# Half of a diagonal block read back turned instead of formed, and another order of steps, in an attention and expert kernel

## The chip, the cores and the metric

The kernel runs on one core of a Trainium2 chip. The metric is the device time of one execution in microseconds; a time is the median of several runs. The engines are named as in the profile: PE is TensorE's matmul side and PEld its weight loads, ACT is ScalarE, DVE is VectorE, POOL is GpSimd, and SP is SyncE, which here issues nearly all DMAs.

## The reference

A batch of 8 sequences of 2496 rows goes through an attention with squared ReLU and no softmax; its output goes, row by row, to one of 8 experts. All of it is float32.

```python
scores = (1.0 / S) * np.matmul(z, z.transpose(0, 2, 1))   # z: 8 x 2496 x 64
attn = np.maximum(scores, 0.0) ** 2
x = (u * np.matmul(attn, v)).reshape(B * S, D)            # D = 256
logits = x @ w_gate + modality_bias[modality_id]
e_idx = np.argmax(logits, axis=1)
# for the rows of each expert e:
out[mask] = gate_w[mask, None] * (np.maximum(x[mask] @ w1[e], 0.0) @ w2[e])
```

The scores come from z on both sides, so the matrix of squares is symmetric: block (q, c) is block (c, q) turned.

## The kernel before

The kernel has two stages. The first, up to about 1287 us, does the attention and the routing; the second runs the experts over tiles of 512 rows and is not touched by the change.

**Tiling of the attention.** A sequence is cut into `NCH` = 5 chunks of 512 queries (the last one 448). Within a chunk (b, c) there are `NI` = 10 steps; step i covers two tiles of 128 keys, 2i and 2i + 1, and so half of key chunk i // 2. Steps 2c and 2c + 1 of chunk c are the diagonal block, where query chunk and key chunk are the same.

**What a step does.** A step that is formed fresh goes through these pieces: `scores` (line 300) makes six matmuls on PE, three for each of the two row halves of the array, with 64 rows of z as weights and up to 512 query columns; `root` (line 317) takes the ReLU out of PSUM on ACT into a tile from the pool `a` (six buffers, named r); `square` (line 359) squares it there. Then `high` (line 386) casts it to ah on ACT or DVE, `low` (line 395) makes the rest al on DVE, and `weigh` (line 409) multiplies ah and al with the two parts of V in 24 matmuls (line 425) that add up in the accumulators acc. The pools ah and al have four buffers each. The score pool s in PSUM has one.

**Squares that are read back.** For key chunks below the query chunk (q < c) the squares have been formed already, in chunk q, with queries and keys the other way round. There, `turn_squares` (line 334) transposes the tile on DVE in blocks of 32 into one of two buffers turn, and `store_squares` (line 342) writes it in four DMAs (six for the last step) to `squares[q, c]` in DRAM. In chunk c, `load_turned` (line 325) reads it back in place of scores, root and square. `turns` says for which pairs this is done.

**Order.** `order_of` (line 277) sets the order of the steps of a chunk: turned steps, called late, and fresh ones are spread evenly among each other, with step 9 last. For chunks 0 to 3 that is

```
chunk 0: 0 1 2 3 4 5 6 7 8 9
chunk 1: 2 0 3 4 5 6 1 7 8 9
chunk 2: 0 4 5 1 6 2 7 3 8 9
chunk 3: 0 6 1 2 7 3 4 8 5 9
```

The order of instructions on each engine is written by a planner that runs when the kernel is built (lines 1120 to 1197). Each piece has an engine, a cost in us, a due time `need` counted in steps, the pieces that it comes after, and the buffers that it takes and gives back. The planner keeps a clock for each engine and gives an engine the piece with the earliest due time that is ready by these clocks. Scores are due `LEAD` = 3.6 steps ahead of their products, and a turned read 2.5 steps before that. SP issues DMAs in the order so planned, through eight lanes: a DMA waits until the one eight places earlier has landed.

## Time and profile before

| what | value |
|---|---|
| median of 3 runs | 2191.28 us (2191.19 to 2193.09) |
| the profiled execution's own time | 2189.61 us |
| its span, first to last instruction | 2187.7 us |
| PE, DVE, ACT busy in the span | 2168.1, 1612.7, 1404.0 us |
| score matmuls (line 314) | 1452 records, 217.3 us busy |
| products (line 425) | 9360 records in three groups of 3120 |
| DMA queue of SP (q1) | 329.58 MB, 58.8% of the 16 engines' span |

The busy time of PE includes matmuls that overlap, and their ends are modelled; what a matmul costs is read from the distance of starts. Matmuls on 64 rows run in pairs, one in each row half of the array. A row of the list of waits names who waited, for whom, and for how long in total, how often, and at the longest.

### The profile page before, as it was taken

To read this page: it belongs to the slowest core of one execution; us is meant where nothing else is said; L and a number is where in the kernel's file an instruction comes from. 1 tells how busy PE (TensorE), PEld (TensorE's weight loads), DVE (VectorE), ACT (ScalarE), POOL (GpSimd) and SP (SyncE) were. 2 spreads that over 40 slices of the span, in tenths; PEclk is the share of its full clock that TensorE was granted. 3 is DMA by queue.
4 is the path that set the end of the run, shared out by engine and by line. 5 is a ranking of instruction groups with operands and counts; after the bars stand their busy time and mean duration, and the time that the engine had idled before them with its cause. 6 is when DMAs were issued, how large, how long until landed. Compare 5 with 4: busy or idle time off the path is not lost. (4 is left out here: it accounts for less than half of the span.)

```text
span 2187.7 us, 42980 instructions
## 1 busy us (share of the span) xinstructions
PE 2168.1 (99%) x16550; PEld 1879.4 (86%) x16550; DVE 1612.7 (74%) x2231; ACT 1404.0 (64%) x1978; POOL 360.3 (16%) x342
## 2 busy tenths in 40 slices
PE   9999999999999999999999999999999999999997
PEld 7888888899998898888888888888888888888886
DVE  8779768778878878778788756666666666666664
ACT  8768768768768677678778753555455555555553
POOL 0000310300300300301302403212121211111121
PEclk9999999999999999999999999999999999999999
DMA  7975976967958958957948833645454544545450
GB/s 176 256 208 119 249 216 145 250 203 155 281 162 176 277 150 180 294 137 168 274 117 173 208 105 102 178 122 168 116 163 127 150 139 135 155 129 161 124 159 24
DMA packets 587874, 373.63 MB, mean 171 GB/s; under 512 B 488426, under 2 KB 543210, under 8 KB 581898
## 3 DMA queue, kind: packets, MB, share of 16 engines
q1 hardware_dynamic: 572570, 329.58, 58.8%
q0 software_dynamic: 15088, 41.21, 5.0%
q8 instruction: 132, 2.16, 0.4%
q14 instruction: 84, 0.69, 0.1%
HBM read 246.49 MB, written 140.96 MB: 177 GB/s over the span
## 5 line engine op out<-in xcount | busy, mean ns | idle before, releaser
L401 DVE TENSOR_TENSOR al<-r,ah 128x1024 fp32r<-128x1024 f32 (+1 forms) x359 | 424.3, 1190 | 56.3 <-ACT ah L392 52.0
L425 PE MATMUL acc<-ah,vh 64*128 64x512 f32 (+1 forms) x3120 | 451.2, 386 | 0.1
L1237 PE MATMUL po<-w,hh 128*128 128x512 f32 x1248 | 448.2, 396 | 2.3 <-issue 2.3
L425 PE MATMUL acc<-al,vh 64*128 64x512 f32 (+1 forms) x3120 | 439.4, 382 | 0.0
L425 PE MATMUL acc<-ah,vl 64*128 64x512 f32 (+1 forms) x3120 | 438.5, 383 | 0.0
L1228 ACT ACTIVATE hh<-ph 128x512 fp32r<-128x512 f32 x312 | 186.1, 597 | 379.4 <-PE ph L1224 379.3
L1224 PE MATMUL ph<-xh,w 128*128 128x512 f32 x1248 | 427.2, 393 | 0.6 <-DVE x L485 0.6
L1229 DVE SCALAR_TENSOR_TENSOR hl<-ph,hh 128x512 fp32r<-128x512 f32 x312 | 215.6, 691 | 230.6 <-ACT hh L1228 230.5
L640 POOL DMA_INDIRECT xs<-x,sloti x160 | 202.5, 1266 | 1064.9 <-ACT ah L392 772.0
L322 ACT ACTIVATE r<-s 128x1024 f32<-128x1024 f32 (+2 forms) x244 | 247.0, 1013 | 173.1 <-PE s L314 166.8
L425 PEld LDWEIGHTS acc<-al,vh 64*128 64x128 f32 x3120 | 319.6, 185 | 40.8
L425 PEld LDWEIGHTS acc<-ah,vh 64*128 64x128 f32 x3120 | 317.1, 185 | 43.5 <-ACT x L481 0.7
L1238 PE MATMUL po<-w,hl 128*128 128x256 f32 x1248 | 350.4, 281 | 0.1
L425 PEld LDWEIGHTS acc<-ah,vl 64*128 64x128 f32 x3120 | 313.6, 185 | 41.9
L392 ACT CAST ah<-r 128x1024 fp32r<-128x1024 f32 (+1 forms) x268 | 272.5, 1031 | 32.0 <-PE acc L425 26.4
L1237 PEld LDWEIGHTS po<-w,hh 128*128 128x128 f32 x1248 | 234.7, 188 | 57.1 <-issue 2.7
L1224 PEld LDWEIGHTS ph<-xh,w 128*128 128x128 f32 x1248 | 234.7, 188 | 55.3 <-PE ph L1224 1.0
L1247 POOL DMA_INDIRECT out_dram<-y,ids x157 | 152.7, 973 | 752.7 <-DVE y L1275 725.6
L368 ACT ACTIVATE r<-r 128x1024 f32<-128x1024 f32 (+2 forms) x243 | 255.9, 1054 | 6.0
L1224 PE MATMUL ph<-xl,w 128*128 128x512 f32 x624 | 245.8, 394 | 0.3 <-DVE xl L866 0.3
L1238 PEld LDWEIGHTS po<-w,hl 128*128 128x128 f32 x1248 | 235.5, 189 | 9.6 <-DVE hl L1229 0.4
L339 DVE STREAM_TRANSPOSE turn<-r 128x1024 f32<-128x1024 f32 x158 | 196.0, 1241 | 45.8 <-ACT r L368 27.7
(159 smaller groups left out, 2177.3 us busy)
## 6 DMA issues: line engine op xcount, KB each, us to landing
squares<-turn SPq DMA_DIRECT2D x508, 128.0 KB
r<-squares SPq DMA_DIRECT2D x96, 512.0 KB
w<-w1s SPq DMA_DIRECT2D x37, 1024.0 KB
w<-w2s SPq DMA_DIRECT2D x37, 1024.0 KB
r<-squares SPq DMA_DIRECT2D x62, 448.0 KB
ut<-in_ut_dram SPq DMA_DIRECT2D x40, 512.0 KB
xg<-xs SPq DMA_DIRECT2D x156, 128.0 KB
vr<-in_v_dram SPq DMA_DIRECT2D x32, 512.0 KB
```

The costliest lines, as they stand in the source:

```text
L322: nc.scalar.activation(out=r[:, t, :w], in_=s[t][:, :w] if g < 2 else s[:, :, :w], func=AF.Relu, scale=INV)
L339: nc.vector.transpose(out=y.rearrange(order, n=2), in_=st_a[g].rearrange("p n (t i) -> p n t i", i=BLK))
L368: nc.scalar.square(out=a[:, t, :w], in_=r[:, t, :w])
L392: copy(out=ah[:, :, :w], in_=st_a[g][:, :, :w])
L401: nc.vector.tensor_tensor(out=al[:, :, :w], in0=a[:, :, :w], in1=ah[:, :, :w].bitcast(F32), op=ALU.subtract)
L425: nc.tensor.matmul(out=acc[b, c][r][dh][:, :w], lhsT=V[b, k // J][y][halves[r], k % J, dh * P:(dh + 1) * P], rhs=x[halves[r], k % 2, :w], ...
L640: nc.gpsimd.indirect_dma_start(out=xs, out_offset=bass.IndirectOffsetOnAxis(ap=RT[b]["sloti"][:n, k:k + 1], axis=0), in_=x[:n, j, :], in_o ...
L1224: nc.tensor.matmul(out=ph, lhsT=lhs, rhs=rhs[:, k, :], start=n == 0, stop=n == 3 * KD - 1)
L1228: nc.scalar.activation(out=hh, in_=ph, func=AF.Relu)
L1229: nc.vector.scalar_tensor_tensor(out=hl, in0=ph, scalar=0.0, in1=hh.bitcast(F32), op0=ALU.max, op1=ALU.subtract)
L1237: nc.tensor.matmul(out=po[j], lhsT=hh[:, s], rhs=both, start=f == 0, stop=False, skip_group_check=True)
L1238: nc.tensor.matmul(out=po[j][:, 0:D], lhsT=hl[:, s], rhs=w[:, 0, :], start=False, stop=f == KF - 1, skip_group_check=True)
```

## The change

The pairs (c, c) for c = 0 to 3 get a place in DRAM too. In those chunks, but for chunk 0 of the first batch, the two diagonal steps no longer do the same work. The first one, 2c, is the source: it is formed whole, and the half of its query columns that belongs to the keys of the other step (columns 256 to 511) is transposed and stored. The second one, 2c + 1, is halved: `scores`, `root` and `square` make only columns 256 to 511, and `load_turned` reads columns 0 to 255 into the same tile. `high`, `low` and `weigh` then work on the whole tile as before. A halved step therefore has both a read and scores.

The order of steps changes with it: the source comes first or second in its chunk and the halved step stands seventh.

```
chunk 0: 0 2 3 4 5 6 1 7 8 9
chunk 1: 0 2 4 5 6 1 3 7 8 9
chunk 2: 0 4 1 6 2 7 5 3 8 9
chunk 3: 0 6 1 2 3 4 7 8 5 9
```

The due times of the source's transpose and stores are moved ahead (n - 1.5 and n - 1.4 instead of n + 0.5 and n + 0.4, counted from its own step n).

```diff
@@ -69,6 +69,7 @@
     w1s = dram.tile([E, P, KD, F], F32, name="w1s")
     w2s = dram.tile([E, P, KF, D], F32, name="w2s")
     places = dram.tile([MAXT, 2], I32, name="places")
+    pairs |= {(c, c) for c in range(NCH - 1)}
     squares = {(q, c, e): dram.tile([T, T], F32, name=f"squares{q}_{c}_{e}") for q, c in pairs for e in range(2)}
 
 
@@ -270,16 +271,27 @@
 
 
     NI = NCOL // 2
+    HALF_AT = 6
 
     def turns(b, q, c):
         return q < c and (q, c) in pairs and (b < B - 1 or q < NCH - 2)
 
+    def halved(b, c):
+        return c < NCH - 1 and b + c > 0
+
     def order_of(b, c):
 
         late = [i for i in range(NI) if turns(b, i // 2, c)]
         fresh = [i for i in range(NI - 1) if i not in late]
-        n = len(late) + len(fresh)
-        return sorted(late + fresh, key=lambda i: (late.index(i) + 0.4) / len(late) if i in late else (fresh.index(i) + 0.6) / len(fresh)) + [NI - 1]
+        at = {i: (n + 0.4) / len(late) for n, i in enumerate(late)}
+        at.update({i: (n + 0.6) / len(fresh) for n, i in enumerate(fresh)})
+        order = sorted(at, key=at.get)
+        if halved(b, c):
+            order.remove(2 * c)
+            order.remove(2 * c + 1)
+            order.insert(1 if late else 0, 2 * c)
+            order.insert(HALF_AT, 2 * c + 1)
+        return order + [NI - 1]
 
     steps = [(b, c, i) for b in range(B) for c in range(NCH) for i in order_of(b, c)]
     first_step = {(b, c): order_of(b, c)[0] for b in range(B) for c in range(NCH)}
@@ -293,6 +305,17 @@
             return x[:, j * P:(j + 1) * P]
         return x[:, j // 2 * H:(j // 2 + 1) * H].rearrange("p (k n) -> p n k", n=2)[:, j % 2]
 
+    def is_half(g):
+        b, c, i = steps[g]
+        return halved(b, c) and i == 2 * c + 1
+
+    def is_source(g):
+        b, c, i = steps[g]
+        return turns(b, c, i // 2) or halved(b, c) and i == 2 * c
+
+    def columns(g):
+        return slice(H if is_half(g) else 0, width[steps[g][1]])
+
     def is_turned(g):
         b, c, i = steps[g]
         return i // 2 < c and turns(b, i // 2, c)
@@ -300,7 +323,7 @@
     def scores(g, more=False):
 
         b, c, i = steps[g]
-        w = width[c]
+        w = columns(g)
         if more:
             s = [bank_tile([P, T], "s") for _ in halves]
         else:
@@ -311,21 +334,24 @@
             for t in range(2):
                 k = 2 * i + t
                 lhs = key_columns(Z[b, k // J][halves[t], kl], k)
-                nc.tensor.matmul(out=s[t][:, :w], lhsT=lhs, rhs=mv[halves[t], ql, :w], start=n == 0, stop=n == 2)
+                nc.tensor.matmul(out=s[t][:, w], lhsT=lhs, rhs=mv[halves[t], ql, w], start=n == 0, stop=n == 2)
         st_s[g] = s if more or not g else both
 
     def root(g):
-        w = width[steps[g][1]]
+        w = columns(g)
         s = st_s.pop(g)
-        r = bulk.tile([P, 2, T], F32, tag="a", bufs=NA, name="r") if g else first_root
+        if is_half(g):
+            r = st_a[g]
+        else:
+            r = bulk.tile([P, 2, T], F32, tag="a", bufs=NA, name="r") if g else first_root
         for t in range(2) if g < 2 else (slice(0, 2),):
-            nc.scalar.activation(out=r[:, t, :w], in_=s[t][:, :w] if g < 2 else s[:, :, :w], func=AF.Relu, scale=INV)
+            nc.scalar.activation(out=r[:, t, w], in_=s[t][:, w] if g < 2 else s[:, :, w], func=AF.Relu, scale=INV)
         st_s[g] = r
 
     def load_turned(g):
 
         b, c, i = steps[g]
-        w = width[c]
+        w = H if is_half(g) else width[c]
         a = bulk.tile([P, 2, T], F32, tag="a", bufs=NA, name="r")
         src = squares[i // 2, c, b % 2].rearrange("(s p k) q -> s p k q", s=2, k=2)
         nc.sync.dma_start(out=a[:, :, :w], in_=src[i % 2, :, :, :w])
@@ -336,7 +362,9 @@
         b, c, i = steps[g]
         y = raw.tile([P, T // BLK, 2 * BLK], F32, tag="turn", bufs=2, name="turn")
         order = "p t (i n) -> p n t i" if i < NI - 1 else "p t (n i) -> p n t i"
-        nc.vector.transpose(out=y.rearrange(order, n=2), in_=st_a[g].rearrange("p n (t i) -> p n t i", i=BLK))
+        t = slice(H // BLK if i == 2 * c else 0, T // BLK)
+        x = st_a[g].rearrange("p n (t i) -> p n t i", i=BLK)
+        nc.vector.transpose(out=y.rearrange(order, n=2)[:, :, t], in_=x[:, :, t])
         st_t[g] = y
 
     def store_squares(g):
@@ -348,7 +376,8 @@
             mine = y[n * BLK:(n + 1) * BLK]
             if i < NI - 1:
                 k0 = i % 2 * H + n * 2 * BLK
-                nc.sync.dma_start(out=dst[:, :, k0:k0 + 2 * BLK], in_=mine)
+                t = slice(H // BLK if i == 2 * c else 0, T // BLK)
+                nc.sync.dma_start(out=dst[:, t, k0:k0 + 2 * BLK], in_=mine[:, t])
             else:
                 for k in range(2 if n < 2 else 1):
                     k0 = (J // 2 + k) * P + n * BLK
@@ -357,7 +386,7 @@
     roots = {}
 
     def square(g):
-        w = width[steps[g][1]]
+        w = columns(g)
         a = r = st_s.pop(g)
         if g < 2:
 
@@ -365,7 +394,7 @@
             roots[g] = r
         for t in (range(2),) if g else ((0,), (1,)):
             t = slice(t[0], t[-1] + 1)
-            nc.scalar.square(out=a[:, t, :w], in_=r[:, t, :w])
+            nc.scalar.square(out=a[:, t, w], in_=r[:, t, w])
         st_a[g] = a
 
     def first_high(g):
@@ -890,7 +919,7 @@
         return p
 
     def piece(on, us, need, f, *args, after=(), take=(), drop=(), gate=-1):
-        p = Piece(on, us, need, f, args, [d if isinstance(d, tuple) else (d, 0.1) for d in after if d], list(take), drop, gate)
+        p = Piece(on, us, need, f, args, [d for d in (d if isinstance(d, tuple) else (d, 0.1) for d in after) if d[0]], list(take), drop, gate)
         pieces.append(p)
         return p
 
@@ -949,34 +978,37 @@
         b, c, i = steps[n]
         f = scale[c]
         high_after = None
-        hold_a = Hold("a", 1 + turns(b, c, i // 2))
-        if is_turned(n):
-            src = [stored[b, i // 2, 2 * c + k] for k in range(2)]
-            p = transfer(1.4, n - LEAD - 2.5, load_turned, n, after=src, take=[hold_a], gate=n - LEAD - 4)
-            high_after = (p, 0.2)
-        elif n >= MADE:
+        hold_a = Hold("a", 1 + is_source(n))
+        read = None
+        if is_turned(n) or is_half(n):
+            src = [stored[b, i // 2, 2 * c + k] for k in range(1 if is_half(n) else 2)]
+            read = transfer(0.7 if is_half(n) else 1.4, n - LEAD - 2.5, load_turned, n, after=src, take=[hold_a], gate=n - LEAD - 4)
+            high_after = (read, 0.2)
+        if not is_turned(n) and n >= MADE:
+            f /= 1 + is_half(n)
             hold_s = Hold("s")
             p = piece(
                 "P", 0.69 * f, n - LEAD, scores, n, after=[done_z.get((b, c)), done_z.get((b, i // 2)), scored.get("last")],
                 take=[hold_s], drop=[hold_z[k] for k in {(b, c), (b, i // 2)}],
             )
             scored["last"] = (p, 0.0)
-            p = piece("A", 0.95 * f + 0.06, n - LEAD + 0.3, root, n, after=[(p, 0.25)], take=[hold_a], drop=[hold_s])
+            p = piece("A", 0.95 * f + 0.06, n - LEAD + 0.3, root, n, after=[(p, 0.25), (read, -20.0)], take=() if read else [hold_a], drop=[hold_s])
             p = piece("A", 0.95 * f + 0.06, n - LEAD + 1.0, square, n, after=[p])
+            f = scale[c]
             high_after = (p, 0.08)
         if n > 0:
             own = n in (1,)
             p = piece(
                 "D" if own else "AD", 1.3 if own else 0.93 * f, n - 1.8, high, n,
-                after=[high_after, split.get("high")], take=[Hold("ah")],
+                after=[high_after, (read, 0.2), split.get("high")], take=[Hold("ah")],
                 drop=[Hold("a")] if n == 1 else (),
             )
             split["high"] = (p, 0.0)
             hold_h = [p.take[0], Hold("al")]
-            if turns(b, c, i // 2):
+            if is_source(n):
                 hold_t = Hold("turn")
-                t = piece("D", 1.18, n + 0.5, turn_squares, n, after=[high_after], take=[hold_t], drop=[hold_a])
-                stored[b, c, i] = transfer(2.8, n + 0.4, store_squares, n, issues=4 if i < NI - 1 else 6, after=[t])
+                t = piece("D", 0.62 if i == 2 * c else 1.18, n - 1.5 if i == 2 * c else n + 0.5, turn_squares, n, after=[high_after], take=[hold_t], drop=[hold_a])
+                stored[b, c, i] = transfer(1.4 if i == 2 * c else 2.8, n - 1.4 if i == 2 * c else n + 0.4, store_squares, n, issues=4 if i < NI - 1 else 6, after=[t])
                 later.append((stored[b, c, i], hold_t))
                 begun.append(stored[b, c, i])
             p = piece(
@@ -1141,7 +1173,7 @@
             need = {}
             for h in p.take:
                 need[h.pool] = need.get(h.pool, 0) + 1
-            if p.f in (load_turned, root) and free["a"] <= sum(n not in held for n in range(step_now + 1, p.args[0])):
+            if p.f in (load_turned, root) and p.args[0] not in held and free["a"] <= sum(n not in held for n in range(step_now + 1, p.args[0])):
                 return False
             return all(free[k] >= n for k, n in need.items())
 
```

How the change stands on the engines, at three places of the fifth batch (b = 4). The rows have the line, the instruction, its output and inputs by the program's names, and its shape; lines of the changed kernel are some twenty to thirty higher. On PE, chunk 0, the seventh group of score matmuls of that chunk, before:

```order
L425 MATMUL acc<-al,vh 128x512 x8
L314 MATMUL s<-zm 128x512 x6
L425 MATMUL acc<-ah,vh 128x512 x8
L425 MATMUL acc<-ah,vl 128x512 x8
L425 MATMUL acc<-al,vh 128x512 x8
L314 MATMUL s<-zm 128x512 x6
```

and now:

```order
L454 MATMUL acc<-al,vh 128x512 x8
L337 MATMUL s<-zm 128x256 x6
L454 MATMUL acc<-ah,vh 128x512 x8
L454 MATMUL acc<-ah,vl 128x512 x8
L454 MATMUL acc<-al,vh 128x512 x8
L337 MATMUL s<-zm 128x512 x6
```

The six matmuls there have 256 columns instead of 512; the products around them are the same in number and shape. On SP, around the end of chunk 2 and the first half of chunk 3 (r is a tile of squares, vr, ut and w1s are the loads of V and U and the laying out of the experts' weights), before:

```order
L355 DMA squares2_4_0_66<-turn_11006 32x16x32 x6
L331 DMA r_11049<-squares2_3_0_78 128x1024
L157 DMA vr_11082<-in_v_dram 128x1024
L331 DMA r_11129<-squares2_3_0_78 128x1024
L157 DMA vr_11132<-in_v_dram 128x1024
L268 DMA ut_11145<-in_ut_dram 128x1024
L218 DMA w1s_61<-in_moe_w1_dram 16x4096
L331 DMA r_11226<-squares0_4_0_70 128x2x448
```

and now:

```order
L384 DMA squares2_4_0_66<-turn_11079 32x16x32 x6
L357 DMA r_11164<-squares2_3_0_82 128x1024
L219 DMA w1s_61<-in_moe_w1_dram 16x4096
L380 DMA squares3_3_0_86<-turn_11188 32x8x64 x4
L158 DMA vr_11230<-in_v_dram 128x1024
L158 DMA vr_11249<-in_v_dram 128x1024
L357 DMA r_11276<-squares2_3_0_82 128x1024
L269 DMA ut_11290<-in_ut_dram 128x1024
L219 DMA w1s_61<-in_moe_w1_dram 16x4096
L357 DMA r_11319<-squares3_3_0_86 128x2x256
L357 DMA r_11373<-squares0_4_0_70 128x2x448
```

The four stores of the source (squares3_3, 8 blocks of 32 instead of 16) and the read of the half are new; five other DMAs stand between them. On DVE, chunk 3, before (turn is a transpose, al a low part, x and rl belong to the output of the chunk before, lg to the routing):

```order
L534 TENSOR_REDUCE lg_10384<-sums_11228 128x32
L638 COPY x_9555<-side_10237 128x2
L339 STREAM_TRANSPOSE turn_11304<-r_11294 128x2x512
L401 TENSOR_TENSOR al_11334<-r_11294,ah_11302 128x1024
L401 TENSOR_TENSOR al_11340<-r_11129,ah_11332 128x1024
L339 STREAM_TRANSPOSE turn_11381<-r_11375 128x2x16x32
L403 TENSOR_TENSOR al_11411<-r_11375,ah_11379 128x512
```

and now:

```order
L531 TENSOR_TENSOR rl_11321<-x_11215,rh_11288 128x1024
L667 COPY x_9670<-side_10270 128x2
L430 TENSOR_TENSOR al_11328<-r_11164,ah_11317 128x1024
L563 TENSOR_REDUCE lg_10477<-sums_11375 128x32
L421 CAST ah_11438<-r_11319 128x1024
L430 TENSOR_TENSOR al_11441<-r_11319,ah_11438 128x1024
L367 STREAM_TRANSPOSE turn_11469<-r_11435 128x2x512
L430 TENSOR_TENSOR al_11475<-r_11435,ah_11443 128x1024
L430 TENSOR_TENSOR al_11481<-r_11276,ah_11473 128x1024
```

The cast of the halved step's tile r_11319, which needs the read, stands on DVE, and its low part, the transpose of the next step and that step's low part come after it. In the whole program there are 186 score matmuls of 256 columns and 1158 of 512 (1344 of 512 before), 31 transposes of half size, and 115 casts of ah on DVE (130 before) beside 283 on ACT (268 before).

## The prediction

> **What bounds the kernel now.** I read the page first, then the list of TensorE's waits, then the busy time of one batch split into its five chunks (each stretch begins at a chunk's first product), and last the timeline of TensorE.
>
> ```profile
> span 2187.7 us, 42980 instructions
> PE 2168.1 (99%) x16550; PEld 1879.4 (86%) x16550; DVE 1612.7 (74%) x2231; ACT 1404.0 (64%) x1978; POOL 360.3 (16%) x342
> ...
> PE po L1237 <- issue: 2.3, 1, 2.3
> PE s L314 <- ACT zm L230: 1.9, 1, 1.9
> PE warm L1101 <- POOL zeros L101: 1.0, 1, 1.0
> PE s L314 <- DVE zm L235: 0.6, 1, 0.6
> PE ph L1224 <- DVE x L485: 0.6, 1, 0.6
> PE ph L1224 <- DVE xl L866: 0.3, 1, 0.3
> ```
>
> Busy 99% alone would prove little, since ends of matmuls are modelled; the six waits do. In the whole span PE waited 6.7 us, and none of it for the pieces ah and al of the attention's squares, nor for a read of turned squares. The chunks of the fourth batch:
>
> ```profile
> 492.30:527.80 35.50, 35.50 (x329) 35.19 (x328) 31.45 (x41) 31.09 (x43) 0.00 (x0) 1.00 0.78 164
> 527.80:561.30 33.50, 33.50 (x316) 33.50 (x314) 27.88 (x47) 28.45 (x37) 7.19 (x6) 1.00 0.81 186
> 561.30:593.10 31.80, 31.80 (x298) 31.80 (x297) 25.87 (x36) 21.57 (x30) 10.68 (x9) 1.00 1.02 292
> 593.10:623.50 30.40, 30.40 (x286) 30.40 (x285) 22.09 (x28) 15.66 (x24) 9.08 (x7) 1.00 0.86 251
> 623.50:652.60 29.10, 29.10 (x299) 29.10 (x297) 23.25 (x28) 22.11 (x33) 0.00 (x0) 1.00 0.39 128
> ```
>
> After the length come PE, PEld, DVE, ACT, POOL, the granted clock and the DMA share. PE is full in all five at a clock of 1.00. DVE is nearest behind it in chunk 0 (31.45 of 35.50), and the DMA engines are full in chunk 2. So **time taken from PE's stream in the attention stage is time taken from the kernel**, as long as operands stay ahead. Whether the stream itself is dense, the timeline tells (start, length, form, count):
>
> ```profile
> 577.80 0.33 PE L514 MATMUL po<-mover,rh 64*128 64x80 f32 x2
> 577.91 0.33 PE L514 MATMUL po<-mover,rl 64*128 64x80 f32 x2
> 578.02 1.00 PE L314 MATMUL s<-zm 64*128 64x512 f32 x6
> ...
> 581.53 0.89 PE L314 MATMUL s<-zm 64*128 64x512 f32 x6
> 582.21 1.12 PE L425 MATMUL acc<-ah,vh 64*128 64x512 f32 x8
> ...
> 584.93 1.12 PE L425 MATMUL acc<-ah,vh 64*128 64x512 f32 x8
> 585.84 1.12 PE L425 MATMUL acc<-ah,vl 64*128 64x512 f32 x8
> ...
> 1700.26 0.28 PE L1238 MATMUL po<-w,hl 128*128 128x256 f32 x1
> 1700.38 0.40 PE L1237 MATMUL po<-w,hh 128*128 128x512 f32 x1
> ```
>
> Starts count here, not lengths. Six score matmuls, three pairs in the two row halves, take 582.21 - 581.53 = 0.68 us: 0.227 a pair. Eight products take 0.91, the same 0.227. No gap is left to win except by fewer columns.
>
> **The change, part by part.** *Scores.* The second diagonal step of chunks 0 to 3, without chunk 0 of the first batch, forms 256 columns: 8 x 4 - 1 = 31 steps, 93 pairs. The order has them as 186 matmuls of 128x256 and leaves all other matmuls in number and shape. No row shows a pair of 64-row matmuls of 256 columns, so it is bounded. From below by the pair of 80 columns, two loads included: 577.91 - 577.80 = 0.11 us. From above by the full width's own 0.227, no gain. The row nearest in width is the 256-column matmul over 128 rows: 1700.38 - 1700.26 = 0.12 us. The trace thus has the same column count at 0.12, and the same number of loads at 0.11; **I take 0.118**. A pair saves 0.109 us, a step 0.327, and 31 steps **10.1 us**; with 0.11 it would be 10.9, at the upper end 0.
>
> The pair's two weight loads are what could spoil this. The Trainium skill (TensorE: Matmul & The Clock Gate, section LDWEIGHTS (loading the stationary operand)) says that a load's time goes by columns, not rows: columns over 1.2, an estimate of 107 ns for 128. Two such loads in a row would hold a pair at 213 ns, and by that rule the sum would be 93 x 0.013 = 1.2 us. The trace disagrees where it can: in the 80-column rows two matmuls with two loads start every 0.11 us, so the loads of the two row halves overlap there.
>
> *ScalarE and VectorE.* The groups by line:
>
> ```profile
> L401 DVE TENSOR_TENSOR al<-r,ah 128x1024 fp32r<-128x1024 f32 (+1 forms) x359 | 424.3, 1190 | 56.3 <-ACT ah L392 52.0
> L322 ACT ACTIVATE r<-s 128x1024 f32<-128x1024 f32 (+2 forms) x244 | 247.0, 1013 | 173.1 <-PE s L314 166.8
> L392 ACT CAST ah<-r 128x1024 fp32r<-128x1024 f32 (+1 forms) x268 | 272.5, 1031 | 32.0 <-PE acc L425 26.4
> L368 ACT ACTIVATE r<-r 128x1024 f32<-128x1024 f32 (+2 forms) x243 | 255.9, 1054 | 6.0
> L339 DVE STREAM_TRANSPOSE turn<-r 128x1024 f32<-128x1024 f32 x158 | 196.0, 1241 | 45.8 <-ACT r L368 27.7
> ```
>
> A halved step takes half of a root and of a square from ACT, about 0.51 + 0.53 = 1.0 us, 32 in all, which I cost at nothing gained since PE never waited for it. The high and low parts stay whole. DVE gains 31 half transposes, between 0.62 (half of 1.241) and 1.24 us each; by size I take 0.62: 19 us over the stage. PE's own work covers it. In chunk 0 DVE goes from 31.45 of 35.50 to 32.1 of 35.2, 91%; at the upper end 93%. That producers run ahead shows in L392: 26.4 of its 32.0 us of idling ended with PE's products, which free the ah buffers. If the cover went, the price would be at most the transposes, 19 us, less the ACT time that the planner can hand over; the order already has 15 casts of ah moved from DVE to ACT (115 instead of 130 on DVE), 15 x 0.68 us back by DVE's rate.
>
> *DMAs.* Each halved step adds four stores of 64 KB and one read of 256 KB, 155 issues on SP. It adds a chain as well: the read needs the stores of the source step of the same chunk. What SP and the lanes give:
>
> ```profile
> 611.64 2.21 SPq L351 DMA_DIRECT2D squares<-turn  x4
> ...
> r<-squares SPq DMA_DIRECT2D x5, 512.0 KB
> squares<-turn SPq DMA_DIRECT2D x12, 128.0 KB
> vr<-in_v_dram SPq DMA_DIRECT2D x2, 512.0 KB
> zr<-in_zt_dram SPq DMA_DIRECT2D x3, 256.0 KB
> squares<-turn SPq DMA_DIRECT2D x10, 64.0 KB
> w2s<-in_moe_w_dram SPq DMA_DIRECT2D x2, 256.0 KB
> ut<-in_ut_dram SPq DMA_DIRECT2D x1, 512.0 KB
> ...
> SPq L331 <- DMA squares<-turn: 7.9, 13, 2.1
> ACT ah L392 <- DMA r<-squares: 1.2, 2, 0.6
> ```
>
> The seven rows in the middle are SP's issues in the fullest stretch, chunk 2: 35 in 31.8 us. With eight lanes at most eight are in flight, so a transfer is in flight 8 x 31.8 / 35 = 7.3 us on average at most. The chain, with its upper ends: root 1.01, square 1.05, transpose 1.24, four issues 2.21, flight of the stores 7.3, flight of the read 7.3, cast 1.03, low part 1.19: 22.3 us. Against it stands PE's work between the source's scores and the halved step's first product. It is shortest in chunk 3; there the order has 93 pairs of products, 16 of 80 columns, 6 of full scores and 3 of half ones: 21.1 + 1.8 + 1.4 + 0.35 = 24.6 us. The low part comes eight pairs (1.8 us) later still. **So the read is hidden, by 2 us where it is tightest**; in chunks 0 to 2 the same count gives about 26 us or more. What remains is that SP stands at the read until the stores have landed, with the next stores behind it; reads that waited for stores so far did it 13 times, 2.1 us at worst. The two turn buffers, and DVE's next transpose, wait behind those stores. I take nothing for it, from a bound of 31 x 2.1 us of SP time, because PE has DVE's lead before it.
>
> *Order.* The first step of chunks 1 is now a turned one, and the source comes second. From a step's scores to its first product PE has as much work between as before (6.1 us at the least then, 6.5 now, by counting the order's rows). That is worth nothing, within 2 us.
>
> *Sum.* 2189.61 us of the profiled execution less 10.1 is 2179.5. The median of the three runs lies 1.7 above that execution, so the forecast is 2191.28 - 10.1 = **2181.2 us**.
>
> **The rivals.** *Loads bind.* The loads of a 64-row pair run one behind the other where matmuls are short. By the 128-row row, one load and its matmul every 0.12 us, two are 0.24, over the 0.227 of a full pair: nothing is gained, 2191.3 us; halfway, at 0.17 a pair, it would be 2186. For it: that row is the only one of 256 columns. Against it: the 80-column pairs. The Trainium skill's rule on weight loads (TensorE: Matmul & The Clock Gate), weighed above, speaks for this rival.
>
> *The reads come late.* The one that ends slower. The DMA engines are at 1.02 and 0.86 in chunks 2 and 3, and there the change adds 0.5 MB each to 292 GB/s x 31.8 us = 9.3 MB and 251 x 30.4 = 7.6 MB. If stores and read each fly 3 us longer, the chain to the cast's end is 28.3 - 1.2 = 27.1 against 24.6 and about 26: the 8 products of chunk 3 start 2.5 us late, the 8 of chunk 2 1.1 us, 29 us together, and the time is 2210. It is slower by more than 0.2% from 14.5 us on (10.1 eaten, 4.4 over), 0.9 us of lateness in each. For it: the full share. Against it: all 158 reads of before made ACT wait 1.2 us in total, and chunk 4, at 0.39, lets the queue drain.
>
> *Operands come later here and there.* A lead that shrinks by a step in chunk 0, where DVE is fullest, or in chunk 3: 0.6 us in each of the 8 batches, 5 us, 2186. Against it: the 26.4 us above.
>
> *The change doesn't do what it says*: excluded, since the order has the 256-column matmuls, half transposes and half reads, and no root in it waits for the read of its own tile.
>
> **How the numbers follow.** A measurement of this kernel tells about 0.2%, 4.4 us, from no change. Forecast 0.72; operands late 0.13; loads bind 0.09; reads late 0.06. The forecast alone spans 2180 to 2183 (10.9 to 8.5 us). Faster takes the forecast and most of the third case, 0.83; same takes the loads and a rest, 0.12; slower 0.05, as the reads may also be late by less. The range, 2179 to 2187, adds the third case and the spread of the runs, and leaves the other two out.
>
> **What would show it.** Right: scores of 256 columns that start 0.35 us before what follows; PE's list of waits still without ah, al and r<-squares; chunks 0 to 3 shorter by 0.33 us each, and chunk 4 and everything behind 1287 us as long as before. Wrong in the first term: 0.6 us or more from a half score to the next product. Wrong in the cover: a wait of PE for ah or al, with DVE or ACT behind the DMA r<-squares, in chunk 3 first.

## The result, and the profile after

| | before | changed |
|---|---|---|
| median, us | 2192.94 (6 runs, 2191.19 to 2193.32) | 2212.91 (6 runs, 2211.24 to 2215.42) |
| ratio | 1 | 1.0093, 95% interval 1.0080 to 1.0106 |
| span of the profiled execution, us | 2187.7 | 2211.8 |
| first product of the second stage at, us | 1293.5 | 1315.6 |

The change makes the kernel slower by 0.9%; the forecast was 2181.2, faster by 0.5%. Of the 24.1 us in the span, 22.1 arise in the attention stage (which before ends at about 1293, not at 1287) and 2.0 behind it. Most of the 2.0 is a stretch of 3.4 us at 1323.8 in which the profile shows the granted clock at half; before has none at that place.

The page of the changed kernel begins so:

```profile
span 2211.8 us, 43316 instructions
...
PE 2173.1 (98%) x16550; PEld 1894.3 (86%) x16550; DVE 1618.4 (73%) x2247; ACT 1392.4 (63%) x1993; POOL 347.1 (16%) x342
```

PE's share falls by one point only. The list of waits shows more (who waited, for whom, us in total, times, longest):

```profile
ACT ah L421 <- DMA r<-squares: 31.7, 10, 7.9
...
DVE turn L367 <- DMA squares<-turn: 29.6, 24, 3.8
...
DVE ah L421 <- DMA r<-squares: 11.8, 6, 4.2
...
PE s L337 <- ACT r L348: 9.1, 9, 1.3
...
PE po L543 <- DVE rl L531: 3.9, 4, 1.6
...
PE po L543 <- ACT sums L556: 2.0, 1, 2.0
...
PE acc L454 <- ACT ah L421: 1.1, 1, 1.1
...
PE acc L454 <- DVE al L430: 0.4, 1, 0.4
```

The casts of ah now wait 31.7 + 11.8 us for reads, where ACT waited 1.2 before. PE itself waits hardly at all for ah and al (1.5 us), but for s and po, which it never waited for in this way before. (po belongs to the output of the chunk before: x is taken out of acc and multiplied with U, ACT casts it to rh, DVE makes the rest rl, PE turns both into po with 80 columns, and ACT copies x and sums out of po.)

The chunks of the fourth batch, as they were shown of before (length, then PE, PEld, DVE, ACT, POOL, granted clock, DMA share, GB/s):

```profile
502.60:539.50 36.90, 35.90 (x334) 29.78 (x332) 32.68 (x51) 32.98 (x47) 0.00 (x0) 1.00 0.87 178
539.50:571.70 32.20, 32.20 (x306) 26.97 (x304) 27.48 (x41) 23.62 (x32) 9.12 (x8) 1.00 0.84 212
571.70:603.20 31.50, 31.50 (x300) 26.37 (x298) 24.70 (x36) 21.71 (x30) 11.09 (x9) 1.00 1.02 294
603.20:633.30 30.10, 30.10 (x287) 28.36 (x285) 20.42 (x23) 17.63 (x27) 3.31 (x4) 1.00 0.92 252
633.30:663.10 29.80, 29.80 (x306) 28.23 (x304) 24.11 (x29) 23.12 (x35) 0.00 (x0) 1.00 0.51 142
```

In this batch chunks 2 and 3 are shorter by 0.3 us each (31.80 and 30.40 before), just as forecast. Chunk 0 is longer by 1.4 (35.50), and PE is idle for 1.00 of it; chunk 1 is shorter by 1.3 (33.50), with ten matmuls fewer in it. The forecast 0.33 us is there where nothing disturbs it; the loss lies in certain chunks.

To find it I took the start of every matmul in the trace and summed, for each chunk, what the distance to the next start exceeds the usual one for its form (113.2 ns for 512 columns, 101 for 448, 59 for 256, 55.5 for 80, 30 for others). These sums are called **gaps** below; they include time at a lower clock. Over the eight batches, in us:

| | chunk 0 | 1 | 2 | 3 | 4 | all |
|---|---|---|---|---|---|---|
| before | 4.6 | 3.2 | 1.5 | 1.3 | 3.8 | 14.5 |
| changed | 10.9 | 5.2 | 4.3 | 21.7 | 4.4 | 46.6 |

The gaps grow by 32.1 us, the score columns give 10.1: 22.0 together, the stage's 22.1. This sum closes because the gaps are what the usual distances leave over; that the saving came is shown by the groups of 256 columns themselves, 0.35 us each (further below). Three times as much was lost. Of the 32.1 us, 6.8 come from three stretches in the attention stage, 13.7 us in all, in which the granted clock is at half; before has none. (Both kernels have one more as the first chunk begins.) Two thirds of the loss lie in chunk 3, and there in few batches: 3.2, 1.3, 4.4, 0.1, 1.9, 1.1, 9.5 and 0.1 us in batches 1 to 8. The seventh shows how. Its chunk 3, in the window lists of before and of the changed kernel:

```profile
1073.90:1104.30 30.40, 30.40 (x286) 25.51 (x284) 19.83 (x25) 19.73 (x28) 6.60 (x6) 1.00 0.89 266
```

```profile
1086.60:1126.10 39.50, 35.82 (x286) 33.55 (x285) 23.80 (x31) 15.92 (x25) 6.91 (x7) 0.87 0.72 199
```

SP's queue in the timeline of the changed kernel (start, length, DMA, number of issues):

```profile
1085.29 7.87 SPq L384 DMA_DIRECT2D squares<-turn  x6
1093.26 2.16 SPq L380 DMA_DIRECT2D squares<-turn  x4
1095.51 0.42 SPq L158 DMA_DIRECT2D vr<-in_v_dram  x1
1095.97 1.55 SPq L357 DMA_DIRECT2D r<-squares  x2
```

The source's transpose ended at 1087.64, but its four stores are issued from 1093.26 on: six stores of another tile (chunk 2's last step) stand ahead of them, and SP spends 7.87 us on those. Two of the six take 1.93 us (from 1086.35) and 3.26 us (from 1089.36); the others take 0.45 to 0.98. It is not their lanes that hold these two: the DMAs eight places ahead of them had landed by 1085.23 and 1086.80, as far as the trace has their signals (16 of 16 and 14 of 16). What holds SP there, the trace doesn't show. The half read goes out at 1097.0 as the second of the last row. Then ACT:

```profile
1094.18 1.05 ACT L525 CAST rh<-x 128x1024 fp32r<-128x1024 f32 x1 [2.29 <-DVE x L521]
1103.09 1.04 ACT L421 CAST ah<-r 128x1024 fp32r<-128x1024 f32 x1 [7.86 <-DMA r<-squares]
1104.04 0.37 ACT L555 COPY x<-po 128x256 f32<-128x256 f32 x1
1104.31 0.22 ACT L556 COPY sums<-po 128x64 f32<-128x64 f32 x1
```

ACT stands 7.86 us at the halved step's cast. Behind it stand the copies out of po, whose products PE started before 1098. And PE, which needs po empty:

```profile
1101.06 1.48 PE L454 MATMUL acc<-al,vh 64*128 64x512 f32 x8
1104.58 0.69 PE L543 MATMUL po<-mover,rh 64*128 64x80 f32 x2 [2.04 <-ACT sums L556]
...
1107.63 2.11 PE L454 MATMUL acc<-ah,vh 64*128 64x512 f32 x8
1109.34 2.11 PE L454 MATMUL acc<-ah,vl 64*128 64x512 f32 x8
1111.05 1.70 PE L454 MATMUL acc<-al,vh 64*128 64x512 f32 x8
1112.47 1.20 PE L454 MATMUL acc<-ah,vh 64*128 64x512 f32 x8
1113.39 1.20 PE L454 MATMUL acc<-ah,vl 64*128 64x512 f32 x8
```

Eight products here start 1.71 us apart (1109.34 - 1107.63) until about 1112, then 0.92 again: the clock is halved after the wait. The halved step's own first product comes only at 1115.9, 12.8 us after its cast began. **In this wait PE did not need the halved tile; it waited for other work that stood behind that tile's cast.** The same is seen in three traces of the experiments below, where the halved step's cast stood on ACT for 7.9 us (another tile in the read), 8.1 (the routing later) and 7.6 (less other traffic, without the first batch), and PE waited 3.6, 2.0 and 2.8 us for sums or r right behind it.

Not all of the loss goes this way. The 9.5 us of this chunk are two waits of PE, each with a stretch at half clock: 1.6 us for rl at 1097.1 with 3.4 us at half clock, and the 2.0 us above with 6.8. The first does not stand behind that cast; it leads back along DVE:

```profile
1086.93 0.71 DVE L367 STREAM_TRANSPOSE turn<-r 128x512 f32<-128x512 f32 x1 [1.75 <-DMA squares<-turn]
...
1095.87 1.22 DVE L531 TENSOR_TENSOR rl<-x,rh 128x1024 fp32r<-128x1024 f32 x1
```

From the source's transpose, which had waited 1.75 us for the stores of an earlier tile, DVE works without a pause up to rl. The third batch's 4.4 us are of this kind too: PE waits 0.9 us for rh and 1.0 for rl, with 3.4 us at half clock, behind a transpose that waited 1.5 us; the halved step's cast doesn't wait there at all. That the transposes' place is what made rl late is read from these traces and was not tested by itself.

### The profile page after: what moved, and what is told of

Its sections match the earlier page's. It is cut to its first block, busy times and chain, and to the rows that moved or that the text cites. A ratio compares the mean times of both kernels' runs of the same rounds, so it can differ in the third digit from the quotient of the medians.

```text
span 2211.8 us, 43316 instructions
## 1 busy us (share of the span) xinstructions
PE 2173.1 (98%) x16550; PEld 1894.3 (86%) x16550; DVE 1618.4 (73%) x2247; ACT 1392.4 (63%) x1993; POOL 347.1 (16%) x342
## 5 line engine op out<-in xcount | busy, mean ns | idle before, releaser
L454 PE MATMUL acc<-ah,vh 64*128 64x512 f32 (+1 forms) x3120 | 479.0, 388 | 2.2 <-ACT ah L421 1.1
L454 PE MATMUL acc<-ah,vl 64*128 64x512 f32 (+1 forms) x3120 | 465.5, 384 | 0.0
L454 PE MATMUL acc<-al,vh 64*128 64x512 f32 (+1 forms) x3120 | 463.3, 383 | 0.4 <-DVE al L430 0.4
L454 PEld LDWEIGHTS acc<-al,vh 64*128 64x128 f32 x3120 | 343.3, 185 | 38.1 <-DVE al L430 1.2
L454 PEld LDWEIGHTS acc<-ah,vh 64*128 64x128 f32 x3120 | 338.9, 186 | 41.8 <-ACT x L510 3.8
L454 PEld LDWEIGHTS acc<-ah,vl 64*128 64x128 f32 x3120 | 339.8, 185 | 38.2
L669 POOL DMA_INDIRECT xs<-x,sloti x160 | 189.4, 1184 | 1099.2 <-ACT r L397 384.9
L421 ACT CAST ah<-r 128x1024 fp32r<-128x1024 f32 (+1 forms) x283 | 287.4, 1033 | 59.6 <-DMA r<-squares 31.7
L348 ACT ACTIVATE r<-s 128x1024 f32<-128x1024 f32 (+2 forms) x244 | 234.2, 961 | 143.5 <-PE s L337 109.5
L367 DVE STREAM_TRANSPOSE turn<-r 128x1024 f32<-128x1024 f32 (+1 forms) x189 | 218.0, 1154 | 59.6 <-DMA squares<-turn 29.6
L397 ACT ACTIVATE r<-r 128x1024 f32<-128x1024 f32 (+2 forms) x243 | 243.0, 1000 | 5.6
```

Source lines behind the costliest of these rows:

```text
L348: nc.scalar.activation(out=r[:, t, w], in_=s[t][:, w] if g < 2 else s[:, :, w], func=AF.Relu, scale=INV)
L367: nc.vector.transpose(out=y.rearrange(order, n=2)[:, :, t], in_=x[:, :, t])
L397: nc.scalar.square(out=a[:, t, w], in_=r[:, t, w])
L421: copy(out=ah[:, :, :w], in_=st_a[g][:, :, :w])
L454: nc.tensor.matmul(out=acc[b, c][r][dh][:, :w], lhsT=V[b, k // J][y][halves[r], k % J, dh * P:(dh + 1) * P], rhs=x[halves[r], k % 2, :w], ...
L669: nc.gpsimd.indirect_dma_start(out=xs, out_offset=bass.IndirectOffsetOnAxis(ap=RT[b]["sloti"][:n, k:k + 1], axis=0), in_=x[:n, j, :], in_o ...
```

## The experiments

Diffs are against the changed kernel. Times are medians; ratios are to runs of before on the same chip.

### First round: the read, the order, the place

*Another tile in the read.* The halved step reads squares that were stored much earlier, so that it depends on no store of its own chunk; its output is therefore not that of the reference.

```diff
-        src = squares[i // 2, c, b % 2].rearrange("(s p k) q -> s p k q", s=2, k=2)
+        q, k, e = i // 2, c, b % 2
+        if is_half(g):
+            q, k, e = (0, c, e) if c else (0, 1, 1 - e)
+        src = squares[q, k, e].rearrange("(s p k) q -> s p k q", s=2, k=2)
```

> The instruction order of the change on every engine and the same DMAs, but the halved step reads squares that were stored a chunk or a batch earlier (of another pair), so the read waits for no store of its own chunk; the squares of the first 256 columns are then other data. Late-read theory (the cast of the halved step stands in its engine's queue before its read has landed, and PE waits for what stands behind it): the casts' waits for r<-squares fall from 43 us to under 10, chunk 3 loses its 20 us of gaps, 2212.9 - 20 - 3 = about 2190. Traffic theory (the 155 added DMAs load the queues, whatever they wait for): 2210 to 2215. Order theory (the new order of steps costs by itself): 2210 to 2215.

Measured: 2211.84 us, ratio 1.0093 (1.0076 to 1.0110); gaps 38.1 in the profiled execution (2206.57 us), 13.6 of them in chunk 3; ACT's casts still wait 26.0 us for reads and DVE's 15.3. The order on SP was unchanged, so the read still stood behind the stores. The time is that of the traffic and order theories, and the casts still wait 41 us instead of under 10. What follows: the dependence on the stores isn't what makes the reads late; with it gone they are as late, at the same place in SP's queue.

*The order alone.* The new order of steps; nothing halved, stored or read in addition.

```diff
+    def cut(b, c):
+        return False
+
     def is_half(g):
         b, c, i = steps[g]
-        return halved(b, c) and i == 2 * c + 1
+        return cut(b, c) and i == 2 * c + 1
...
-        return turns(b, c, i // 2) or halved(b, c) and i == 2 * c
+        return turns(b, c, i // 2) or cut(b, c) and i == 2 * c
```

> The new order of steps alone: no step is halved, no diagonal square stored or read, all scores 512 wide. Late-read theory: about the time of before, 2190 to 2196, with gaps of PE as before (14.5 us in the attention stage). Traffic theory: the same, 2190 to 2196. Order theory: the 32 us of new gaps stay and the 10 us of narrower scores are not had, 2220 to 2225.

Measured: 2193.96 us, ratio 1.0011 (1.0001 to 1.0020), gaps 17.3. The order by itself costs about 2 us; the order theory (2220) is out. In this run DVE's transposes wait 25.7 us for stores, nearly as long as in the changed kernel (29.6), and PE loses almost nothing by it.

*Chunks 0 to 2 only*, with the old order in chunk 3:

```diff
-        return c < NCH - 1 and b + c > 0
+        return c < NCH - 2 and b + c > 0
```

> The change in chunks 0 to 2 alone; chunk 3 has its old order and two full diagonal steps. Late-read theory: chunk 3's 20.4 us of new gaps go, and 8 x 0.33 = 2.6 us of narrower scores with them: 2212.9 - 20.4 + 2.6 = 2195. Traffic theory: 8 of 31 halved steps gone, so a quarter of the 32 us: 2212.9 - 8 + 2.6 = 2207. Order theory: 2195 too if chunk 3's order is what costs, so that order_only has to tell these apart.

Measured: 2190.81 us, ratio 0.9995 (0.9986 to 1.0005), gaps 23.3. Leaving chunk 3 out takes 22 us off, more than the late-read theory said (2195) and far from the traffic theory's 2207. But the 7.5 us that 23 halved steps should bring are eaten: 8.8 us of gaps more than before, 4.4 of them in chunk 2 of the first batch.

*A cast planned later.* The planner puts the halved step's cast 6 us after it believes the read to have landed, so that other work goes ahead of it.

```diff
-            high_after = (read, 0.2)
+            high_after = (read, 6.0 if is_half(n) else 0.2)
...
-                after=[high_after, (read, 0.2), split.get("high")], take=[Hold("ah")],
+                after=[high_after, (read, 6.0 if is_half(n) else 0.2), split.get("high")], take=[Hold("ah")],
```

> The change with one number of the planner raised: the cast of a halved step may be put in its queue only 6 us after the planner's landing of its read, instead of 0.2. Same computation, same DMAs. Late-read theory: other work passes the cast, the waits for r<-squares fall below 15 us, and the time comes to 2185 to 2197. Traffic and order theories: 2208 to 2216, since neither the DMAs nor the order of steps are changed.

Measured: 2217.46 us, ratio 1.0116 (1.0099 to 1.0133); 30.3 us of gaps in chunk 3. The expectation failed, and the time is above the range of the two other theories as well. The trace shows why: ACT's wait for reads fell from 31.7 to 20.6 us, but in six of the eight chunks 3 the halved step's first product now starts within 1.1 us of its cast's end, and PE waits for ah, 4.7 us (cast on DVE) and 2.9 (on ACT). Chunk 3 has no room for the chain: put the cast early and it blocks, put it late and its product is late.

### Second round: blocked casts, traffic, and the routing

*The read kept, but used by nobody.* Scores, root and square of the halved step are formed at full width; the half read lands in a scratch place.

```diff
     def columns(g):
         b, c, i = steps[g]
-        return slice(H if is_half(g) else 0, width[steps[g][1]])
+        return slice(0, width[steps[g][1]])
...
-        nc.sync.dma_start(out=a[:, :, :w], in_=src[i % 2, :, :, :w])
+        out = aside[b, c] if is_half(g) else a[:, :, :w]
+        nc.sync.dma_start(out=out, in_=src[i % 2, :, :, :w])
```

> The order of the changed kernel to the row, with the same stores and the same 31 half reads; but the halved steps form all 512 score columns and their root and square at full width, and the half read lands in a scratch place of its own that no instruction uses. Theory A (the cast of the halved step stands in the in-order queue of ACT or DVE until its read lands, and the work behind it, above all the copies out of po, comes late to PE): the waits ah <- DMA r<-squares fall from 31.7 (ACT) and 11.8 us (DVE) to below 3 each, the 20 us of extra gaps in chunk 3 go, the 10.1 us of score columns come back: 2212.9 + 10.1 - 20.4 = about 2203 us. Rival B (the added transfers themselves, in lanes and in SP's queue, delay every other read and store): the gaps stay, and the time is 2212.9 + 10.1 = 2223 us.

Measured: 2208.98 us, ratio 1.0074 (1.0059 to 1.0089). The casts' wait for reads is gone from both engines' lists but for one row:

```profile
PE s L338 <- ACT r L349: 8.6, 8, 1.3
...
ACT ah L423 <- DMA r<-squares: 3.2, 2, 2.2
```

Chunk 3's gaps fall from 21.7 to 10.3, and in batches 2 to 8 from 18.5 to 4.4. On ACT, DVE and SP the instructions of the attention stage stand in the same order as in the changed kernel, and the transfers are much the same: in chunk 3 the half read flies 6.9 us (7.1) and has landed 22.0 us (22.8) after the source's root began. So what the use of the read costs in those batches is 14.1 us of the 17.7 by which they exceed before; this is theory A. The 5.8 us left in the first batch and the 10.6 in chunk 0 are something else; hence 2209 and not 2203. Theory B (2223), the transfers as the whole cause, is out.

*Chunk 3 only.*

```diff
-        return c < NCH - 1 and b + c > 0
+        return c == NCH - 2
```

> The change in chunk 3 alone (8 halved steps, 2.6 us of score columns less). Theory A: chunk 3 has too little work between the source and the halved step, whatever chunks 0 to 2 do, so its gaps stay near 20 us: 2191.7 + 20 - 2.6 = 2209 us. Rival B (a backlog of transfers that builds up over chunks 0 to 2): with no added transfers ahead of it, chunk 3 has less than half of these gaps, and the time is below 2199 us.

Measured: 2198.30 us, ratio 1.0025 (1.0016 to 1.0035), gaps 10.1 in chunk 3. Neither forecast for theory A's size (20) holds, and the bound set for B is met. But the chain from the source's root to the landed read takes 22.1 us on average here, against 22.8 in the changed kernel: no backlog from chunks 0 to 2 lengthens it. The casts now wait 16.0 us on ACT and 3.9 on DVE, less than half; why the same chain blocks them less in this order is not shown. More than half of the 10.1 us (5.4) lie in the first batch.

*The routing later.* In five batches of the changed kernel a row of PE's timeline stood out, at the routing of the batch before (pc are the counts of the experts):

```profile
371.66 1.08 PE L337 MATMUL s<-zm 64*128 64x512 f32 x6
372.43 0.27 PE L633 MATMUL pc<-cnt,below 64*128 64x8 f32 x1
...
373.86 0.98 PE L337 MATMUL s<-zm 64*128 64x512 f32 x6 [0.99 <-ACT r L348]
```

Two groups of scores stand back to back, and with one score buffer the second waits until ACT has taken out the first. Five of PE's nine waits for r in the list are such places, four in chunk 0 and one in chunk 1; the other four lie in chunks 1 to 3 of the first batch. The order of before has no such place, nor has the run with the order of steps alone; the planner makes them when it places the shortened pieces. Due seven steps later, the routing is planned elsewhere:

```diff
-            route_pieces(b, WHOLE if whole else SOON, end + (4 if whole else 2), [p for k in range(c + 1) for p in taken[b, k]])
+            route_pieces(b, WHOLE if whole else SOON, end + (11 if whole else 2), [p for k in range(c + 1) for p in taken[b, k]])
```

> The changed kernel, with the routing of a batch due 7 steps later, so that its counts no longer stand between two groups of scores that follow each other at once. Theory C (the second group waits for the root of the first, 1.2 to 1.9 us, in five batches): chunk 0 falls from 10.9 us of gaps to about 4.5, and chunk 1 loses the 1.8 us of the fourth batch (the fifth by count): 2212.9 - 8 = about 2205 us. Rival (PE would wait for DVE's work of the routing at that place in any order): 2213 us, with the gaps under another name.

Measured: 2198.93 us, ratio 1.0034 (1.0020 to 1.0047); gaps 32.4, with 4.3 in chunk 0 as theory C has it. That is 6.6 us. In chunk 1 the fifth batch falls from 2.0 to 0.6, though the sum over the batches rises from 5.2 to 5.8. Another 7.7 us went out of chunk 3, which the theory didn't foresee: the seventh batch's 9.5 us became 0.1, as the order around its cast had changed too, while the third batch's 4.4 became 5.2. The casts still wait 21.6 us on ACT and 21.8 on DVE.

*Three chunks, without chunks 0 and 2 of the first batch,* and with the later routing:

```diff
-        return c < NCH - 1 and b + c > 0
+        return c < NCH - 2 and (b, c) not in ((0, 0), (0, 2))
```

> The change in chunks 0 to 2 only, without the first batch's chunks 0 and 2 (22 halved steps, 66 pairs x 0.109 = 7.2 us less), and the routing due 7 steps later. If late reads in chunk 3, the first batch's chunk 2 and the groups of scores in a row are all that eats the gain: gaps as before, 2191.7 - 7.2 + 0 to 2 = 2184.5 to 2186.5 us. If the added stores and reads cost something in every chunk: 2190 us or more, as with chunks 0 to 2 alone (2190.8).

Measured: 2187.84 us, ratio 0.9983 (0.9974 to 0.9992): faster than before, and between the two cases, 1.3 us above the upper end of the first. Gaps are 18.9, 4.4 more than before.

### Third round: is it the traffic, or the room in chunk 3?

*Less other traffic in chunk 3.* The 64 copies of expert weights (256 KB each) leave the other chunks and go into chunk 4:

```diff
-        start = per + NI + n * 4
+        start = n // NI * per + (NCH - 1) * NI + n % NI - 2
```

> The version with the late routing, and the 64 copies of expert weights (256 KB each, on SP's queue, till now one every four steps from the second batch on) issued from chunk 4 of the batches only, where the DMA share is lowest. Theory B as the rest of chunk 3's gaps has it (stores and half reads come late because the queue is full with other transfers): the gaps of chunk 3 in batches 2 to 8, 10.8 us in the version with the late routing, fall below 5, and the time from 2198.9 to between 2190 and 2194 us. Rival (the chain from the source is too long by itself, its own stores and the turned reads of chunks 3 and 4 fill the queue): the gaps stay and the time is 2197 to 2201 us.

Measured: 2204.22 us, ratio 1.0060 (1.0037 to 1.0084); chunk 3 has 19.1 us of gaps, 15.9 of them in batches 2 to 8. The copies are not the cause. But the rival doesn't fit either: the time lies 3 us over its range (four runs, 2197.8 to 2210.1), and the chain did get shorter, 20.1 us from the source's root to the landed read instead of 22.7, while chunk 3's gaps grew from 14.0 to 19.1. A shorter chain thus went with larger gaps, in another order of the planner. The casts' longest wait was 6.2 us. Without the first batch (`b > 0` in place of `b + c > 0`):

> The same without the change in the first batch (28 halved steps, 93 - 9 = 84 pairs x 0.109 = 9.2 us less). If the copies are what delays chunk 3: 2191.7 - 9.2 + 4 = 2186.5 us. If not: the gaps of the first batch (7.5 us of the late routing's 32.4, before 3.2) go and the rest stays, 2198.9 - 4.3 + 1.0 = about 2195.5 us.

Measured: 2196.16 us, ratio 1.0023 (1.0014 to 1.0032), as the second case has it. Chunk 3 keeps 13.5 us, mostly in two batches (6.3 and 4.2).

*More room in chunk 3.* With the copies back in place and the later routing, the halved step of chunk 3 becomes the last but one of its ten steps:

```diff
-            order.insert(HALF_AT, 2 * c + 1)
+            order.insert(NI - 2 if c == NCH - 2 else HALF_AT, 2 * c + 1)
```

The expectation calls this one place later; it is two, seventh to ninth.

> The version with the late routing, and in chunk 3 the halved step one place later (last but one of the nine steps). If chunk 3's gaps are lateness of a chain whose length doesn't depend on where its result is used: one step more, about 3 us, for each of the 8 batches, of 14.0 us of gaps in chunk 3 at most 6 stay, and 2198.9 - 8 = about 2191 us. If SP's queue shifts with the step (what stands ahead of the half read comes with the halved step's place): the gaps stay at 10 us or more, 2196 us or above.

Measured: 2188.25 us, ratio 0.9988 (0.9979 to 0.9998), 10.7 us below the version with the later routing alone (on another chip; by the two ratios it is 10.1). Chunk 3's gaps fall from 14.0 to 2.6. From the source's root to the landed read it still takes 22.6 us, but to the halved step's first product there are 31.1 us instead of 26.2. Its list of waits:

```profile
ACT ah L421 <- DMA r<-squares: 27.3, 15, 3.9
...
DVE ah L421 <- DMA r<-squares: 5.2, 4, 2.9
```

The casts still wait often, but at most 3.9 us at a time instead of up to 8.1, and PE hardly waits behind them. This fits long stalls at the head of a queue as the cause, but doesn't prove it: in the changed kernel a stall of 6.9 us cost nothing (eighth batch), and the next run has large gaps without one.

*The same without the first batch:*

> The same without the change in the first batch (28 halved steps, 9.2 us less). With chunk 3's gaps at most 4 us over those of before and chunks 0 to 2 as in the version of three chunks: 2191.7 - 9.2 + 4 + 1 = 2187.5 us, level with that version (2187.8); if the gaps stay at 10 us: 2193.5 us.

Measured: 2191.22 us, ratio 0.9998 (0.9989 to 1.0007), between the two cases. The profiled execution (2193.04 us) is the second case: 11.0 us of gaps in chunk 3, 5.5 of them in the seventh batch and 2.2 in the eighth. In those two the halved step's cast doesn't wait for its read; PE waits for x, al, rh and rl. The room of 4.9 us keeps the casts' waits at 4.5 us or less in both orders, and that is enough in one and not in the other.

## Why the prediction was wrong, point by point

**The score term was right.** A group of 256-column scores among products of the changed kernel:

```profile
1087.99 0.53 PE L337 MATMUL s<-zm 64*128 64x256 f32 x6
1088.34 0.85 PE L454 MATMUL acc<-ah,vh 64*128 64x512 f32 x4
```

Three pairs take 0.35 us, 0.117 a pair; the prediction took 0.118 from rows of 80 columns and of 128 rows. The rival *loads bind* is out, and with it the rule of the Trainium skill (TensorE: Matmul & The Clock Gate, section LDWEIGHTS (loading the stationary operand)) in the form in which it was weighed there: two loads in a row at an estimated 107 ns each would have held the pair at 0.214.

**ScalarE and VectorE were about right.** The groups after:

```profile
L348 ACT ACTIVATE r<-s 128x1024 f32<-128x1024 f32 (+2 forms) x244 | 234.2, 961 | 143.5 <-PE s L337 109.5
...
L367 DVE STREAM_TRANSPOSE turn<-r 128x1024 f32<-128x1024 f32 (+1 forms) x189 | 218.0, 1154 | 59.6 <-DMA squares<-turn 29.6
```

31 half transposes took 218.0 - 196.0 = 22.0 us, 0.71 each for a forecast 0.62. ACT's roots gave back 247.0 - 234.2 = 12.8 us for a forecast 16. The sizes held; where these pieces stand in their queues is another matter.

**The step that failed is "So the read is hidden, by 2 us where it is tightest".** It asked whether the halved step's own product comes late, and put everything else that a late read can do at nothing. The chain of chunk 3, in us, means of its eight instances in the trace of the changed kernel:

| part | forecast | measured |
|---|---|---|
| root and square | 2.06 | 2.1 |
| square's end to the transpose: DVE's queue | 0 | 3.1 |
| transpose | 1.24 | 0.7 |
| transpose's end to the first store: SP's queue | 0 | 4.2 |
| four issues | 2.21 | 1.9 |
| last issue to all stores landed | 7.3 | 2.7 |
| landed to the read's issue | 0 | 0.9 |
| flight of the read | 7.3 | 7.1 |
| sum | 20.1 | 22.8 |

The mean flight bound (7.3) fits the read and is far too long for the stores. The waits in the queues, 3.1 and 4.2 us, were not in the sum at all: the chain was added up as if each engine were free when its turn came. With a cast and a low part (2.2 us) the chain is 25.0 us against the 24.6 that the prediction counted as PE's cover. The cover was counted well: from the source's root to the halved step's first product it is 23.8 to 24.5 us in the four batches with the smallest gaps (2, 4, 6 and 8). The margin of 2 us was gone on average. In chunks 0 and 1 the cast comes 9.1 and 5.6 us after the read has landed; in chunk 2 it comes 0.6 after, in chunk 3 0.2.

Still, the halved step's own product was hardly late. In all eight chunks 3 its cast had ended when that product came, by 0.1 to 11.8 us, and PE's waits for ah and al in the whole kernel make 1.5 us. That wait was the prediction's own sign of an error in the cover, and it stayed away while 22 us were lost.

**What took its place is the wait of the cast at the head of its queue.** The prediction, and its rival *the reads come late*, let only the halved step's product be late, by the chain's overhang. But the cast is placed in ACT's or DVE's queue where the planner expected the read. Its cost model gives a half read on a free queue 0.4 + 0.5 + 0.7 + 1.1 = 2.7 us from issue to landing, where 7.1 were measured. All that stands behind the cast waits as well: copies out of po, low parts, roots. On ACT's timeline above, 7.86 us of standing delayed work that had nothing to do with the diagonal. The Trainium skill says as much of the two queues (TensorE: Matmul & The Clock Gate, section Architectural detail: the array is 16× 32×32, not 1× 128×128): they are strictly first in, first out. The trace agrees: nothing on ACT passed the cast in those 7.86 us. Taking the cast's need of the read away, with the order kept, took 14.1 us of gaps out of chunk 3 in batches 2 to 8. The rival's time, 2210, lay near the result by luck, not by its account: it assumed flights 3 us longer, 2.5 us for each chunk 3 and 1.1 for each chunk 2. In fact chunk 3 lost nothing to 4.4 us in seven batches and 9.5 in one, and chunk 2 lost only in the first batch (3.0).

**"That is worth nothing, within 2 us"**, said of the order, holds for the order alone (about 2 us, 1.0011). It fails in combination. The count went from a step's scores to its own product and didn't look at scores that follow scores: five places at the routing (four in chunk 0, 6.6 us, and one in chunk 1, 1.4 us, shown by moving the routing), and in the first batch the same kind of gap, two of 1.4 us in chunk 2 and one in chunk 3. There another 1.4 us follow, in which PE waits for the halved step's cast, which stands behind its own late root and square; its read had landed 0.8 us before. All of these went away where those chunks were not halved.

**"I take nothing for it"**, the price of the stores on SP, is not settled. SP stands at reads until stores have landed for 24.0 us (41 times) instead of 7.9 (13 times), and DVE's transposes wait 29.6 us for stores instead of 13.7. The order of steps alone has 25.7 us of such waits with gaps of 17.3, so the waits by themselves cost little. In the version whose read nobody uses, of the 35.5 - 14.5 = 21.0 us of added gaps 7.5 lie in chunks 0 and 1 and 9.8 in the first batch's chunks 2 and 3, which have mainly the other causes named above; 3.7 are left that may be the stores' price. In the changed kernel itself the waits for rh and rl in the third and seventh batch may be part of it.

As far as separate runs can be added up, of the 32.1 us of added gaps 14.1 belong to the use of the read in chunk 3, 8.0 to the five places at the routing, and 5.5 to the first batch's chunks 2 and 3; 4.5 are not placed.

What stays open: when a blocked cast costs something. In the eighth batch of the changed kernel ACT stood 6.9 us at the halved step's cast with the same copies out of po behind it, and nothing was lost: PE formed the products in po only from 1268.1 to 1269.3, the cast went on at 1270.0, and the copies were done at 1271.8, 0.6 us before PE needed po again. Two orders with a blocked cast in the seventh batch gave 9.5 and 0.1 us. So it is a matter of when PE needs what stands behind; this was seen, not controlled.

## What to carry to other kernels

A chain that crosses engines is not the sum of its parts: add for each hop the time that the in-order queue is busy with something else, read from the trace for that stage, and a sum of durations with a margin of a tenth proves no cover. Where an instruction may have to wait at the head of an in-order queue, price what stands behind it, by when it is needed next, and not only its own result. When a change shortens some pieces and re-plans the order, look through the new order for users of a single buffer that now follow each other at once.

The version that left out the chunk without room and one that gave the chain room there beat the kernel before by 0.17% and 0.12% (0.9983 and 0.9988), 4.3 of the 7.2 us and 3.0 of the 10.1 us that they take out of the scores. That is at the edge of what these runs tell, and the same room without the first batch was level with before (0.9998).

## What was not expected of the hardware

**Half a clock after short waits.** PE's clock fell to half for stretches of about 3.4 us (449.9 to 453.4, 1098.5 to 1101.9) and 6.8 us (1105.3 to 1112.1) in chunk 3. In the timeline each comes behind waits of PE: 0.9 and 1.0 us one after the other, 1.6 us, and 2.0 us. The second:

```profile
1095.28 0.30 PE L543 MATMUL po<-mover,rh 64*128 64x80 f32 x2
1097.14 0.30 PE L543 MATMUL po<-mover,rl 64*128 64x80 f32 x2 [1.55 <-DVE rl L531]
```

The 3.4 us at half clock behind a wait of 1.6 us thus cost another 1.7 us. The Trainium skill (TensorE: Matmul & The Clock Gate, section HAM oscillation — how this bites in real kernels) asks for no idle gaps of PE above about 3.4 us; here shorter ones were followed by the half clock. The length of a wait doesn't decide it alone. In the first batch's chunk 2 PE waits twice for 1.12 us, 2.1 us apart, in the changed kernel and in the version whose read nobody uses; only in the latter do 3.4 us at half clock follow (at 104.2). With the cast planned later, a wait of 2.05 us (at 141.7) was followed by none.

**A full share of the DMA engines is not a long flight.** In chunk 2, at a share of 1.02, the stores landed 2.8 us after their last issue and the half reads took 4.9 us; in chunk 3, at 0.72 to 0.92, the reads took 7.1. Moving 64 copies of 256 KB out of these chunks made the half read's flight in chunk 3 shorter, 5.5 us instead of 7.0, and its gaps larger.
